# Inverting the softmax sums of couples 6 to 23 as 14 columns over 128 partitions instead of as 448 columns over 128

## The chip, the core and the metric

The kernel runs on one core of a Trainium2 chip. A core has five engines that run their own instruction streams side by side: TensorE (PE, the matrix multiplier, which writes to PSUM only), VectorE (DVE), ScalarE (ACT), GpSimd (POOL) and SyncE (SP), which here does nothing but issue DMAs. Every stream is in order: an instruction that waits for a semaphore holds back all that stand behind it on the same engine. The metric is the device time of one execution in microseconds (us).

## The reference

Attention over 8 batches, 12 heads, 448 positions and head size 64, with q and k normalised by their root mean square, followed by a two-layer network on the 3584 rows (model width 768, inner width 2048):

```python
rms = np.sqrt(np.mean(x * x, axis=-1, keepdims=True) + 1e-06)   # for q and for k, times a gain
scores = (1 / np.sqrt(64)) * np.matmul(q_n, k_n.transpose(0, 1, 3, 2))
attn = np.exp(scores - max);  attn = attn / (sum(attn) + 1e-09)
x = matmul(attn, v)                     # rows (b, s), columns (h, d)
h = x @ w_in                            # 768 -> 2048
out = (h * (1 / (1 + np.exp(-h)))) @ w_out   # 2048 -> 768
```

All in float32. The kernel doesn't subtract the maximum where the gains bound the scores; that is the path that runs (`bounded`).

## The kernel before, in words

**Couples.** Four heads of one batch are a couple (24 couples, 3 per batch; `GROUP` = 6 couples are two batches). For couple c, `visit(c)` computes scores for 128 keys at a time (L752), exponentials on ScalarE (L757), and products with v (L789) that add up in two PSUM banks, `av0` and `av1`, of which there is one buffer each. `between(c)` then prepares the next couple (transposes or `flip` of q and k) and fills TensorE's time with matmuls of the first layer of the network, for the two batches that were finished before: `fill(...)` takes them from a generator (`halves_in`, L963), product by product. Each product of 448 columns goes to a PSUM bank, of the pool `ps_mm` (name `mm`, two buffers) or, by turns, of the pool with the scores (name `sc`, two buffers of two banks). VectorE or ScalarE takes it out; with two buffers, a product into `mm` can start only when the product before the last one in `mm` has been taken out.

**Sums.** The softmax's sum over keys is a matmul with ones. From couple 6 on VectorE first adds the exponentials of the key blocks onto those of block 0 (`add`, L803), so that TensorE has one term left: 4 matmuls of 32 output rows (L832), which give the four heads' sums, each repeated over 32 of the 128 partitions. In couples 6 and 10 (`FULL`) the block of left-over keys wasn't added by VectorE; it is a second term of 4 matmuls.

**Reciprocals.** `invert(half)` (L841) takes the reciprocal of 128 x 224 sums from PSUM, twice, into `r[0]`; `spread` copies it to `r[1]` (L847), and 4 DMAs from SBUF to SBUF (L850, on SP) exchange halves, so that `r[i]` has the factor of each of the 128 rows of x of pair i. `divide(c, sums)` (L863) multiplies the two `av` banks by `r[0]` and `r[1]`, two instructions, and so frees the banks.

**Order.** Nothing but the order in the program decides. For couples 6, 7, 8, 9, 11, 17 and 23 the sums and reciprocals stand in `between(c)`, and `divide(c, sums)` stands in `visit(c + 1)`, ahead of the first product with v of couple c + 1. In the other couples from 10 on (`LAGGED`) the sums stand at the end of `between(c)`, the reciprocals in `visit(c + 1)`, x is copied out undivided (L1526) and divided in `between(c + 1)`. The pieces of `prompt` are put between the fill's products: the first one ahead of them, one more after each product. SP issues everything in order too: loads of q, k and v, of the weights, the stores of the layer's result to DRAM (L1002), and the reciprocals' DMAs.

After couple 23 the rest of the first layer and then the second layer follow, without attention.

## Time and profile before

| | us |
|---|---|
| median of 3 runs | 1294.37 |
| lowest, highest | 1294.12, 1294.78 |
| span of the profiled execution | 1294.6 |
| PE busy | 1283.5 |
| DVE busy | 971.4 |
| ACT busy | 504.3 |
| POOL busy | 363.5 |
| attention with the first layer beside it (up to the last product with v) | about 711 of the span |

The page gives per engine its busy time, the chain of work that ended last and groups of like instructions. Timelines give for one engine the start in us from the span's beginning, the time taken, engine and line, operation, output and inputs, and how often in a row; in brackets how long the engine stood idle ahead of it and who released it. A PE row counts two records for each matmul in float32, so a term of the sums (4 matmuls) is x8. A row of SPq is the issue of DMAs; landing comes later. The granted TensorE clock was 0.999 over the execution.

### The profile page before, as it was taken

The numbers are of one execution on the slowest core, as the hardware profiler recorded it, in microseconds if no ns is written. First come the engines' busy times: TensorE is split into PE (matmuls) and PEld (weight loads), VectorE is DVE, ScalarE is ACT, GpSimd is POOL, SyncE is SP. The second block draws the span as 40 slices with busy tenths as digits, with TensorE's granted clock in tenths as the row PEclk, the third lists the DMA queues.
The fourth block names the chain that finished last, engine by engine and source line by source line (L and its number), as shares of the span: only waits on it lengthen the run. The fifth ranks groups of instructions, "written<-read, shape, count | busy, mean of one in ns | idle before, by whom it ended". The sixth has DMA issues, their size and how long they took to land.

```text
span 1294.6 us, 19931 instructions
## 1 busy us (share of the span) xinstructions
PE 1283.5 (99%) x7212; PEld 840.7 (65%) x7212; DVE 971.4 (75%) x1672; ACT 504.3 (39%) x880; POOL 363.5 (28%) x221
## 2 busy tenths in 40 slices
PE   9999999999999999999999999999999999999998
PEld 4444454444444454444544555559999999999998
DVE  6898878868666558666555886798978787878785
ACT  7967666645555554554543344310001000000000
POOL 6765454543344344343311344400000000000000
PEclk9999999999999999999999999999999999999999
DMA  9675347434444444444411466312332313141411
GB/s 232 174 193 136 104 124 197 95 83 102 112 94 91 119 91 102 108 93 93 107 50 69 149 204 219 117 66 88 100 94 86 113 67 129 51 133 48 141 39 40
DMA packets 266160, 144.15 MB, mean 111 GB/s; under 512 B 203748, under 2 KB 249956, under 8 KB 266052
## 3 DMA queue, kind: packets, MB, share of 16 engines
q1 hardware_dynamic: 265424, 141.68, 39.8%
q8 instruction: 59, 0.97, 0.3%
q0 software_dynamic: 320, 0.90, 0.2%
q14 instruction: 49, 0.40, 0.1%
q10 hardware_dynamic: 308, 0.20, 0.1%
HBM read 95.36 MB, written 41.29 MB: 106 GB/s over the span
## 4 chain that ended last, share of the span: by engine, by line
PE 97%; DVE 1%; POOL 1%; issue 0%; ACT 0%; DMA 0%; SPq 0%; ACTq 0%; DVEq 0%; POOLq 0%
PE alone L1285 23%; PE mm L963 21%; PE sc L963 11%; PE av L789 10%; PE sc L752 10%; PE mm L1285 8%; PE alone L963 7%; PE alone L1323 2%; PE mm L832 2%; PE mm L1323 1%; PE sc L643 1%; PE sc L832 1%; PE sc L674 0%; DVE work L912 0%; POOL rms L503 0%
## 5 line engine op out<-in xcount | busy, mean ns | idle before, releaser
L757 ACT ACTIVATE work<-sc,rms 128x448 f32<-128x448 f32 x318 | 182.0, 635 | 98.0 <-PE sc L752 85.7
L752 PE MATMUL sc<-work 64*64 64x448 f32 x1344 | 169.4, 543 | 1.0 <-ACT work L653 0.6
L789 PE MATMUL av<-work,rows 64*64 64x448 f32 x1272 | 155.5, 540 | 1.2 <-DVE x L1514 0.9
L963 PE MATMUL mm<-x,W 128*128 128x448 f32 x366 | 149.1, 542 | 0.0
L963 PE MATMUL mm<-sums_x,W 128*128 128x448 f32 x348 | 142.4, 542 | 0.0
L803 DVE TENSOR_TENSOR work<-work 128x896 f32<-128x896 f32 (+1 forms) x110 | 118.3, 1105 | 28.6 <-PE av L789 28.1
L530 POOL DMA_DIRECT2D out_dram<-x x2 | 1.2, 592 | 443.5 <-DVE x L912 443.5
L503 POOL TENSOR_TENSOR rms<-rms,minus_half 128x14 f32<-128x14 f32 (+4 forms) x40 | 97.4, 2437 | 86.8 <-DVE rms L499 83.3
L963 PEld LDWEIGHTS mm<-x,W 128*128 128x128 f32 x366 | 68.5, 190 | 70.3 <-issue 64.8
L1285 PE MATMUL alone<-W,rows 128*128 128x192 f32 x610 | 113.0, 326 | 0.0
L963 PEld LDWEIGHTS mm<-sums_x,W 128*128 128x128 f32 x348 | 65.1, 190 | 68.1 <-issue 62.5
L789 PEld LDWEIGHTS av<-work,rows 64*64 64x64 f32 x1272 | 65.9, 132 | 62.8 <-issue 19.3
L752 PEld LDWEIGHTS sc<-work 64*64 64x64 f32 x1344 | 60.4, 132 | 63.3 <-ACT work L757 25.3
L1285 PEld LDWEIGHTS alone<-W,rows 128*128 128x128 f32 x610 | 101.4, 190 | 0.0
L963 PE MATMUL sc<-x,W 128*128 128x448 f32 x246 | 99.6, 541 | 0.0
L984 POOL TENSOR_TENSOR stage<-parts,stage 128x448 f32<-128x448 f32 x31 | 39.8, 1285 | 169.2 <-ACT stage L983 168.9
L722 POOL TENSOR_TENSOR rms<-rms,minus_half 128x28 f32<-128x28 f32 x15 | 72.6, 4842 | 48.9 <-DVE rms L719 47.8
L963 PEld LDWEIGHTS sc<-x,W 128*128 128x128 f32 x246 | 46.4, 190 | 47.0 <-issue 46.7
L1285 PE MATMUL alone<-W,work 128*128 128x192 f32 x382 | 72.2, 326 | 0.0
L1295 ACT COPY rows<-alone 128x192 f32<-128x192 f32 x33 | 10.5, 318 | 141.5 <-PE alone L1285 136.7
L1285 PEld LDWEIGHTS alone<-W,work 128*128 128x128 f32 x382 | 63.8, 190 | 0.0
L1116 ACT ACTIVATE stage<-stage 128x896 f32<-128x896 f32 x63 | 56.8, 945 | 17.1 <-DVE stage L912 16.9
(267 smaller groups left out, 2312.8 us busy)
## 6 DMA issues: line engine op xcount, KB each, us to landing
hidden<-stage SPq DMA_DIRECT2D x63, 448.0 KB, 2.9
work<-hidden SPq DMA_DIRECT2D x21, 1024.0 KB, 5.1
rows<-in_moe_w_out_dram SPq DMA_DIRECT2D x32, 384.0 KB, 3.7
W<-in_moe_w_in_dram SPq DMA_DIRECT2D x22, 512.0 KB, 5.3
x<-hidden SPq DMA_DIRECT2D x7, 1024.0 KB, 6.1
rows<-in_q_dram SPq DMA_DIRECT2D x120, 56.0 KB, 2.2
rows<-in_k_dram SPq DMA_DIRECT2D x120, 56.0 KB, 2.3
rows<-in_k_dram SPq DMA_DIRECT2D x60, 96.0 KB, 2.6
```

The costliest lines, as they stand in the source:

```text
L503: nc.gpsimd.tensor_tensor(out=t, in0=t, in1=half, op=ALU.pow)
L722: nc.gpsimd.tensor_tensor(out=f, in0=f, in1=minus_half.to_broadcast([P, n]), op=ALU.pow)
L752: nc.tensor.matmul(two[ds(half * D, D), h, 0:S], keys[rows, ts(half, D)], qT[rows, pair, :], start=True, stop=True,)
L757: nc.scalar.activation(left_weights(c)[:, h] if j == LEFT else weights(c, j)[:, i, h], two[:, h, 0:S], AF.Exp, scale=norm.column(c, i, h, j),)
L789: nc.tensor.matmul(sums[i][ds(h * D, D), :], v, w, start=(j == 0 and step == 1), stop=(j == LEFT - 1 and step == 1),)
L803: nc.vector.tensor_tensor(out=total, in0=total, in1=more, op=ALU.add)
L832: nc.tensor.matmul(t[ds(h * D + i * n, n), :], ones[:, which + i if which else 0], left_weights(c)[:, h] if which else w()[:, i, h], start ...
L963: nc.tensor.matmul(t, self.left(name, s), self.right(name, s), start=s == ends[0], stop=s == ends[1])
L984: nc.gpsimd.tensor_tensor(out=done[1, 2], in0=u2, in1=p5, op=ALU.add)
L1116: nc.scalar.activation(t, t, AF.Silu)
L1285: nc.tensor.matmul(t, x[:, i], y, start=i == ORDER[0], stop=i == ORDER[-1])
L1323: nc.tensor.matmul(o, a[:, 2 * i + m, t], right_one(name, i)[:, m], start=n == 0, stop=n == len(steps) - 1,)
```

## The change

For c >= 6, `sum_up` gives other pieces. `gather`: ScalarE copies all sums, 128 x 448, from PSUM to `r[0]`, and 4 DMAs take one partition of each group of 32 (448 values, one head) and lay it out as 32 partitions x 14 in a new tile `spot`; the four heads fill 128 partitions. `invert_all`: VectorE takes the reciprocal of `spot`, 128 x 14; one DMA writes it to a DRAM tile `totals` (two of them, by turns), and 4 DMAs read it back, each one head's 448 values repeated over 64 partitions, into `r[0]` and `r[1]`. The second term of couples 6 and 10 goes; VectorE adds the left-over keys there too. Couples 0 to 5 stay as they were.

```diff
-    FULL = (GROUP, SOON - 1)
+    totals = [dram.tile([4, S], F32, name=f"totals{i}") for i in range(2)]
+    spot = mem.tile([P, 4 * S // P], F32, name="spot")
...
-        if c in FULL:
-            terms.insert(0, (1, None))
...
-        yield [lambda: invert(0), lambda: (invert(1), spread())]
+        def gather():
+            nc.scalar.copy(r[0], t)
+            rows = r[0].rearrange("(n p) s -> n p s", n=4)[:, 0]
+            for n in range(4):
+                dst = spot[ts(n, P // 4)]
+                nc.sync.dma_start(dst, rows[n : n + 1].rearrange("n (p e) -> n p e", p=P // 4))
+
+        def invert_all():
+            d = totals[c % 2]
+            nc.vector.reciprocal(out=spot, in_=spot)
+            nc.sync.dma_start(d.rearrange("n (p e) -> (n p) e", p=P // 4), spot)
+            for i in range(2):
+                for h in range(2):
+                    source = d[2 * h + i : 2 * h + i + 1].to_broadcast([D, S])
+                    nc.sync.dma_start(r[i][ts(h, D)], source)
+
+        if c >= GROUP:
+            yield [gather, invert_all] if c in LAGGED else [gather, lambda: None, invert_all]
+        else:
+            yield [lambda: invert(0), lambda: (invert(1), spread())]
...
             if LATE - 1 <= c < NC - 1:
-                reciprocals += [lambda: flip(c + 1, "k"), gain]
+                reciprocals[1] = lambda: flip(c + 1, "k")
+                reciprocals.append(gain)
...
-        late = add(c, LEFT - 1) if c >= GROUP else []
-        if c >= GROUP and c not in FULL:
-            late += add(c, LEFT)
+        late = add(c, LEFT - 1) + add(c, LEFT) if c >= GROUP else []
```

Three places show how this moves instructions. Names: `rows` is the ring of loaded q, k and v, `W` the weights, `stage` and `parts` hold products on their way out, `work` holds `r`.

SP in couple 8, before: the loads of k by rows, the exchange of the reciprocals, the eight loads of k by quarters (which wait for `flip`), then weights and stores.

```order
L287 DMA rows<-in_k_dram 128x3x64 x2
L289 DMA rows<-in_k_dram 64x2x64
L850 DMA work<-work 32x448 x4
L255 DMA rows<-in_k_dram 32x14x32 x8
L88 DMA x_173<-in_moe_w_in_dram 128x512
L1002 DMA hidden<-stage 128x896 x2
```

The same place after the change:

```order
L287 DMA rows<-in_k_dram 128x3x64 x2
L289 DMA rows<-in_k_dram 64x2x64
L862 DMA spot<-work 32x1x14 x4
L255 DMA rows<-in_k_dram 32x14x32 x8
L867 DMA totals_172<-spot 128x14
L871 DMA work<-totals_172 64x448 x4
L88 DMA x_175<-in_moe_w_in_dram 128x512
L1020 DMA hidden<-stage 128x896 x2
```

Four DMAs have become nine, and the eight loads now stand between the first four and the last five. In couples 11 and 17 the order is the same; in couple 9 the two stores to `hidden` stand in between as well; in couple 7 the eight loads stand ahead of all nine.

VectorE in couple 7, second half, before: the two reciprocals and the copy, one piece of weights, the sum of squares (L705), and the first two products taken out of PSUM (L912).

```order
L841 RECIPROCAL work<-sc 128x224 x2
L847 COPY work<-work 128x448
L126 TENSOR_SCALAR W<-W 128x512
L129 TENSOR_SCALAR W<-W 128x512
L133 SCALAR_TENSOR_TENSOR W<-W 128x512
L705 TENSOR_REDUCE rms_61<-rows 128x28
L912 TENSOR_TENSOR parts<-sc,parts 128x448
L912 TENSOR_TENSOR stage<-mm,stage 128x448
```

The same place after the change:

```order
L126 TENSOR_SCALAR W<-W 128x512
L129 TENSOR_SCALAR W<-W 128x512
L133 SCALAR_TENSOR_TENSOR W<-W 128x512
L866 RECIPROCAL spot<-spot 128x14
L930 TENSOR_TENSOR parts<-sc,parts 128x448
L706 TENSOR_REDUCE rms_61<-rows 128x28
L930 TENSOR_TENSOR stage<-mm,stage 128x448
```

The small reciprocal, which needs the four gathers landed, stands ahead of three instructions that didn't wait for a DMA before.

VectorE in couple 6, first half, before: additions of exponentials, one piece of weights, and a product taken out of PSUM.

```order
L803 TENSOR_TENSOR work<-work 128x896 x2
L126 TENSOR_SCALAR W<-W 128x512
L129 TENSOR_SCALAR W<-W 128x512
L133 SCALAR_TENSOR_TENSOR W<-W 128x512
L912 TENSOR_TENSOR parts<-mm,parts 128x448
```

The same place after the change:

```order
L804 TENSOR_TENSOR work<-work 128x896 x2
L804 TENSOR_TENSOR work<-work 64x896 x2
L126 TENSOR_SCALAR W<-W 128x512
L129 TENSOR_SCALAR W<-W 128x512
L133 SCALAR_TENSOR_TENSOR W<-W 128x512
L930 TENSOR_TENSOR parts<-mm,parts 128x448
```

Two additions of 64 x 896 now stand ahead of the product. TensorE's own order is the same before and after, but for the 8 matmuls that go.

## The prediction

> **What bounds the kernel now.** I read the page first, for the engine that is never free, then TensorE's waits, then the timelines of the couples that the change touches, SP and VectorE beside TensorE.

> ```profile
> span 1294.6 us, 19931 instructions
> ...
> PE 97%; DVE 1%; POOL 1%; issue 0%; ACT 0%; DMA 0%; SPq 0%; ACTq 0%; DVEq 0%; POOLq 0%
> ```

> The second line is the chain that ended last, by engine: 97% of the span is TensorE following TensorE. How little it waits is in the view of waits, which for TensorE has 8 rows, of which the first and the last are:

> ```profile
> PE idle L412 <- POOL ident masks.py:199: 1.4, 1, 1.4
> ...
> PE sc L643 <- DVE rows L518: 0.2, 1, 0.2
> ```

> The eight add up to 4.8 us, and only few tenths of that lie beyond the start. So a faster VectorE can give next to nothing by itself; the change can win only what it takes off TensorE, and it loses whatever makes TensorE wait. What has to be asked is how long each new chain of DMAs is, and what stands behind it.

> **What it takes off TensorE.** The sums of couple 6, with two terms, and of couple 7, with one:

> ```profile
> 135.48 1.71 PE L832 MATMUL sc<-work,ones 128*32 128x448 f32 x16
> ...
> 169.56 0.96 PE L832 MATMUL sc<-work,ones 128*32 128x448 f32 x8
> ```

> A term costs 1.71 - 0.96 = 0.75 us. Couples 6 and 10 lose one each: **-1.5 us**.

> **What it takes off and puts on the others.** By groups, and one pair of the added additions as it stands in couple 23:

> ```profile
> L841 DVE RECIPROCAL work<-mm 128x224 f32<-128x224 f32 x24 | 37.0, 1547 | 4.1 <-PE mm L832 4.1
> ...
> L983 ACT COPY stage<-sc 128x448 f32<-128x448 f32 x10 | 5.3, 528 | 20.2 <-PE sc L963 20.2
> ```
> ```profile
> 692.01 2.20 DVE L803 TENSOR_TENSOR work<-work 64x896 f32<-64x896 f32 x2
> ```

> In each of 18 couples VectorE loses two reciprocals of 1.55 us and a copy; the reciprocal of 14 columns is 14/224 of 1.55, 0.1 us, say 0.2 with its overhead. By the waits above this saves TensorE nothing. ScalarE gets a copy out of PSUM, 0.53 us each.

> **The new chain.** The trace has no such DMAs, so I build it from the nearest rows: the exchange that goes, a k load of 96 KB (read from DRAM) and stores to DRAM.

> ```profile
> L850 SPq DMA_DIRECT2D work<-work x74: 513/583/1280, 112.5 to 703.6; - x74
> ...
> DMA to landing us min/median/max: 1.9/2.0/3.8
> ```
> ```profile
> rows<-in_k_dram SPq DMA_DIRECT2D x60, 96.0 KB, 2.6
> ...
> out_dram<-work SPq DMA_DIRECT2D x4, 120.0 KB, 2.1
> ...
> out_dram<-work SPq DMA_DIRECT2D x6, 48.0 KB, 4.2
> ```

> An issue takes SP 0.58 us, four 2.4 us; a small DMA lands 2.0 us after its issue. Four gathers issued from T: the fourth is issued at T + 1.8 and landed at T + 3.8; the reciprocal is done at T + 4.0. The write to DRAM lands 2.0 later (between 1.9 and 4.2, the last row; I take 2.0, as it is nearer in size to the exchange). The four reads (64 x 448 values, 112 KB) wait for it on SP; the fourth is issued 1.8 later and lands after 2.4, between 2.1 and 2.6. So `r` is complete **6.2 us after the write's issue**, 10.2 after T where nothing stands between. The old exchange needed 1.8 + 2.0 after the copy.

> [...]

> Now each place where something waits for this. A divide that starts at D frees `av0` and `av1` for the next products with v. Couple 7's shows the slack:

> ```profile
> 184.59 1.16 DVE L863 TENSOR_TENSOR x<-av,work 128x448 f32<-128x448 f32 x2 [1.34 <-PE av L789]
> ```
> ```profile
> 185.88 0.56 PE L789 MATMUL av<-work,rows 64*64 64x448 f32 x4
> ```

> The first product is at D + 1.3, the one into the second bank 0.38 later, and the divide's second half takes 0.62: it can start at D + 1.0 without holding TensorE.

> Couple 7. SP, VectorE and TensorE:

> ```profile
> 173.31 4.19 SPq L255 DMA_DIRECT2D rows<-in_k_dram  x8
> ```
> ```profile
> 176.51 1.08 DVE L705 TENSOR_REDUCE rms<-rows 128x28 f32<-128x896 f32 x1
> 177.50 0.61 DVE L912 TENSOR_TENSOR parts<-sc,parts 128x448 f32<-128x448 f32 x1
> 178.03 0.61 DVE L912 TENSOR_TENSOR stage<-mm,stage 128x448 f32<-128x448 f32 x1
> ```
> ```profile
> 179.57 0.92 PE L963 MATMUL mm<-x,W 128*128 128x448 f32 x2
> ```

> The gathers stand behind the eight loads: T = 177.5, landed 181.3, reciprocal done 181.5. VectorE holds until then, and behind it stand the three instructions of 0.61, 1.08 and 0.61 us: 183.8. The matmul at 179.57 needs the bank that the third of them empties. **+4.2 us**. `r` is complete at 187.7, against 185.6 + 4.2: no more.

> Couple 8:

> ```profile
> 206.00 0.60 SPq L289 DMA_DIRECT2D rows<-in_k_dram  x1
> ...
> 209.88 4.18 SPq L255 DMA_DIRECT2D rows<-in_k_dram  x8
> ```
> ```profile
> 216.51 1.16 DVE L863 TENSOR_TENSOR x<-av,work 128x448 f32<-128x448 f32 x2 [1.31 <-PE av L789]
> ```

> T = 206.6; gathers to 209.0, eight loads to 213.2, then the write: `r` at 219.4, allowed 217.5. **+1.9**.

> Couple 9, with the two stores between as well:

> ```profile
> 235.56 0.60 SPq L289 DMA_DIRECT2D rows<-in_k_dram  x1
> ...
> 242.32 1.19 SPq L1002 DMA_DIRECT2D hidden<-stage  x2
> ```
> ```profile
> 248.42 1.16 DVE L863 TENSOR_TENSOR x<-av,work 128x448 f32<-128x448 f32 x2 [1.34 <-PE av L789]
> ```

> 236.2 + 2.4 + 4.2 + 1.2 = 244.0; `r` at 250.2, allowed 249.4. **+0.8**.

> Couples 11 and 17, in the order of couple 8:

> ```profile
> 301.75 0.60 SPq L289 DMA_DIRECT2D rows<-in_k_dram  x1
> ```
> ```profile
> 312.84 1.16 DVE L863 TENSOR_TENSOR x<-av,work 128x448 f32<-128x448 f32 x2 [0.28 <-PE av L789]
> ```
> ```profile
> 501.48 0.60 SPq L289 DMA_DIRECT2D rows<-in_k_dram  x1
> ```
> ```profile
> 512.72 1.16 DVE L863 TENSOR_TENSOR x<-av,work 128x448 f32<-128x448 f32 x2 [0.28 <-PE av L789]
> ```

> 302.35 + 2.4 + 4.2 + 6.2 = 315.1, allowed 313.8: **+1.3**. 502.1 + 12.8 = 514.9, allowed 513.7: **+1.2**.

> Couple 6. VectorE is full here, and the two additions stand ahead of a product that TensorE waits for:

> ```profile
> 130.39 1.37 DVE L126 TENSOR_SCALAR W<-W 128x512 f32<-128x512 f32 x1
> ...
> 132.87 0.62 DVE L912 TENSOR_TENSOR parts<-mm,parts 128x448 f32<-128x448 f32 x1
> ...
> 151.18 1.16 DVE L863 TENSOR_TENSOR x<-av,work 128x448 f32<-128x448 f32 x2 [1.29 <-PE av L789]
> ```
> ```profile
> 174.97 0.43 DVE L126 TENSOR_SCALAR W<-W 128x512 f32<-128x512 f32 x1
> ```
> ```profile
> 133.87 0.92 PE L963 MATMUL mm<-sums_x,W 128*128 128x448 f32 x2
> ```
> ```profile
> 145.99 0.86 SPq L1002 DMA_DIRECT2D hidden<-stage  x2
> ```

> 2.2 us more would end that product at 135.7 instead of 133.5. The first of the three weight steps behind the additions took 1.37 us beside a busy GpSimd and 0.43 in couple 7, and starts 2.2 later, when GpSimd is done: about 1.2 us later in all (0 to 2.2). **+1.2**, which eats that couple's 0.75. Its `r`: the write goes out behind the stores, at 146.9 at the latest, complete 153.1, allowed 152.2 plus the 0.4 that TensorE is late by then; the reciprocals that go let the weights and so the stores go earlier, so 0 (0 to 0.5).

> Couple 10 costs nothing: its additions stand where VectorE idles. The lagged couples and the last one:

> ```profile
> 675.88 1.16 ACT L757 ACTIVATE work<-sc,rms 128x448 f32<-128x448 f32 x2 [1.24 <-PE sc L752]
> ```
> ```profile
> 696.53 1.15 DVE L863 TENSOR_TENSOR x<-x,work 128x448 f32<-128x448 f32 x2
> ...
> 711.25 1.16 DVE L863 TENSOR_TENSOR x<-av,work 128x448 f32<-128x448 f32 x2 [1.10 <-PE av L789]
> ```

> Couple 22: gathers from 677.6 (exponentials, then the copy), `r` at 687.8, wanted at 696.5. Couple 23: copy after the divide that ends at 697.7, T = 698.2, `r` at 708.4, wanted at 711.25. Nothing in either; they are hidden by the matmuls of the first layer, and cost only if the chain took over 3 us more.

> **Sum.** -1.5 + 4.2 + 1.9 + 0.8 + 1.3 + 1.2 + 1.2 = +9.1 us, on a span of 1294.6, 0.2 above the median of the runs. On the median, 1294.37: **1303.5**.

> **The rivals.**

> *Slow hops.* If the write to DRAM takes the 4.2 us of the 48 KB stores, `r` is 2.2 later: 8.8 in couples 8, 9, 11 and 17, some 1.4 in couple 6, 0.1 in couple 7: 1313.8. For it speaks that row; against it the other stores, 2.1. Chance 0.15. [...]

> *Short hops.* If write and reads take under 4.3 us instead of 6.2, couples 8, 9, 11 and 17 are free: -1.5 + 1.2 + 4.2, 1298.3. Against it: no row lands under 1.9, and the four issues alone are 2.4. Chance 0.13.

> *Not slower: no wait decides.* One mechanism, the gathers are issued before the eight loads hold them up: SP, freed of L850's waits, runs ahead, so that couple 7's reciprocal is done by 177 and `r` early everywhere. That needs T by 173 in couple 7. Then only the terms count: 1292.9, or 1294.1 with couple 6's additions. Against it: the gathers stand behind the loads in the order, and SP issued these without a gap. Chance 0.10.

> **How the numbers follow.** My forecast, 0.62, has 1300 to 1308 as its own range by the bounds above. For 8 in 10 I reach down into the short hops and up to the slow ones: 1296 to 1313. About 0.2% is what a measurement of this kernel can tell from no change, that is 1291.8 to 1297.0. Slower: the forecast, the slow hops and most of the short ones, 0.85. The same: the last rival and a little of the short hops, 0.13. Faster by more needs 2.6 us, and the terms are 1.5: 0.02.

> **What would show it.** In the new profile: L832 in couples 6 and 10 with x8; a TensorE idle of about 4 us in couple 7's second half, put down to VectorE or to DMA into `spot`; in couples 8, 9, 11 and 17 waits of VectorE's divide for DMA into `work`, with 1 to 2 us of TensorE behind each; 1 us in couple 6; nothing in the lagged couples or in couple 23. It is wrong if these landings are not near 2 us, or if TensorE doesn't need the bank in couple 7.

## The result and the profile after

The changed kernel takes 1325.09 us (median of 5 runs, 1321.37 to 1328.36) against 1294.49 (1294.12 to 1294.78): 1.0238 times as long, 95% interval 1.0222 to 1.0255, **30.6 us slower**. The forecast was 1303.5, its range 1296 to 1313. The sign was right, the size was not: the loss is over three times the 9.1 us of the sum.

The page of the profiled execution (1328.29 us, of which 1326.5 are the span) first: the span, TensorE's busy time, the granted clock by slices, and the chain that ended last.

```profile
span 1326.5 us, 20023 instructions
...
PE 1298.6 (98%) x7196; PEld 840.3 (63%) x7196; DVE 910.6 (69%) x1640; ACT 511.3 (39%) x898; POOL 363.6 (27%) x221
...
PEclk9999889999999999999999999999999999999999
...
PE 86%; DMA 4%; SPq 3%; DVE 2%; ACT 2%; issue 1%; POOL 1%; ACTq 0%; DVEq 0%; POOLq 0%
```

Two things stand out. The chain is TensorE for 86% instead of 97%: DMA, SP and VectorE have come into it, so there are new waits. And TensorE is **busy** for 15.1 us more than before (1298.6 against 1283.5), though it runs 16 matmul records less. Two slices of its clock are at 8 tenths, and the mean granted clock is 0.991 instead of 0.999.

The waits of TensorE, in total per releaser (us in total, times, longest); these are the new rows:

```profile
PE av L790 <- DVE x L881: 11.4, 9, 2.2
PE mm L981 <- DVE stage L930: 3.9, 1, 3.9
PE mm L981 <- DVE parts L930: 1.7, 1, 1.7
...
PE mm L981 <- ACT stage L992: 0.7, 1, 0.7
```

17.7 us, none of which stood in the profile before. In TensorE's timeline the places are these (start, us; in brackets the idle time ahead and the releaser):

```profile
134.21 1.02 PE L981 MATMUL mm<-sums_x,W 128*128 128x448 f32 x2 [1.73 <-DVE parts L930]
...
154.42 1.28 PE L790 MATMUL av<-work,rows 64*64 64x448 f32 x4 [2.12 <-DVE x L881]
...
189.78 1.86 PE L981 MATMUL mm<-x,W 128*128 128x448 f32 x2 [3.86 <-DVE stage L930]
...
235.16 0.59 PE L790 MATMUL av<-work,rows 64*64 64x448 f32 x2 [1.67 <-DVE x L881]
...
269.34 0.97 PE L790 MATMUL av<-work,rows 64*64 64x448 f32 x4 [2.24 <-DVE x L881]
271.40 1.01 PE L790 MATMUL av<-work,rows 64*64 64x448 f32 x2 [1.09 <-DVE x L881]
...
338.12 0.97 PE L790 MATMUL av<-work,rows 64*64 64x448 f32 x4 [1.42 <-DVE x L881]
...
543.47 2.22 PE L790 MATMUL av<-work,rows 64*64 64x448 f32 x6 [1.81 <-DVE x L881]
```

In this order they are couple 6's additions, couple 6's divide, couple 7's bank, and the divides of couples 8, 9 (two rows), 11 and 17. Six of these seven places were named in the prediction with a wait of their own; couple 6's divide was put at nothing.

What lies behind each wait shows in windows of TensorE (from:to, length, busy and records, **granted clock**, DMA share, GB/s):

```profile
154.95:161.78 6.83, 6.51 (x34) 0.50 0.07 15
189.08:195.91 6.83, 6.13 (x30) 0.50 0.25 70
225.00:235.00 10.00, 8.19 (x69) 1.00 0.62 135
271.00:274.41 3.41, 3.01 (x16) 0.50 0.06 14
339.27:342.68 3.41, 3.14 (x18) 0.50 0.08 18
544.07:547.48 3.41, 3.41 (x18) 0.50 0.13 28
```

Behind five of the seven waits TensorE ran at half clock, 0.50, for 3.41 us or for twice that. Reckoned from that clock as half the work, a stretch of 3.41 us costs it 1.7, and the five rows lose 3.4 + 3.4 + 3 x 1.7 = **12 us** at most (11 if only the 22.2 us count in which it was busy there), an estimate. That is why busy time grew: in the timeline above, the two records at 189.78 take 1.86 us at half clock; the same two took 0.92 before. The starts of the five stretches lie 34.13, 81.92, 68.27 and 204.80 us apart, which is 10, 24, 20 and 60 times 3.413: in this execution half clock set in on a grid of 3.413 us, not at the moment in which a wait began or ended (in couple 9 1.66 us after TensorE had started again at 269.34, in couple 7 0.70 us before it did at 189.78).

So of the 31.9 us between the two spans, waits are 17.7 and half clock some 12; the terms give back 1.5, and the first 100 us, whose code is the same, have 1.2 us less idling in this execution (TensorE busy for 96.63 us instead of 95.42). About 5 us remain that neither view places.

### The profile page after: what moved, and what is told of

Read it like the earlier page. It is cut to its first block, busy times and chain, and to the rows that moved or that the text cites. A ratio compares the mean times of both kernels' runs of the same rounds, so it can differ in the third digit from the quotient of the medians.

```text
span 1326.5 us, 20023 instructions
## 1 busy us (share of the span) xinstructions
PE 1298.6 (98%) x7196; PEld 840.3 (63%) x7196; DVE 910.6 (69%) x1640; ACT 511.3 (39%) x898; POOL 363.6 (27%) x221
## 4 chain that ended last, share of the span: by engine, by line
PE 86%; DMA 4%; SPq 3%; DVE 2%; ACT 2%; issue 1%; POOL 1%; ACTq 0%; DVEq 0%; POOLq 0%
PE alone L1303 22%; PE mm L981 16%; PE av L790 9%; PE sc L981 9%; PE sc L753 9%; PE mm L1303 8%; PE alone L981 7%; PE alone L1341 2%; PE mm L831 2%; SPq L255 1%; DMA work<-totals 1%; DMA totals<-spot 1%; PE mm L1341 1%; SPq L871 1%; ACT stage L1134 1%
## 5 line engine op out<-in xcount | busy, mean ns | idle before, releaser
L753 PE MATMUL sc<-work 64*64 64x448 f32 x1344 | 181.7, 558 | 1.1 <-ACT work L654 0.6
L790 PE MATMUL av<-work,rows 64*64 64x448 f32 x1272 | 170.5, 558 | 11.7 <-DVE x L881 11.4
L804 DVE TENSOR_TENSOR work<-work 128x896 f32<-128x896 f32 (+1 forms) x114 | 125.0, 1126 | 43.9 <-PE av L790 43.3
L1002 POOL TENSOR_TENSOR stage<-parts,stage 128x448 f32<-128x448 f32 x31 | 38.9, 1255 | 185.6 <-ACT stage L1001 176.8
L1313 ACT COPY rows<-alone 128x192 f32<-128x192 f32 x33 | 10.5, 318 | 141.3 <-PE alone L1303 141.3
```

What stands on the lines that cost most here:

```text
L753: nc.tensor.matmul(two[ds(half * D, D), h, 0:S], keys[rows, ts(half, D)], qT[rows, pair, :], start=True, stop=True,)
L790: nc.tensor.matmul(sums[i][ds(h * D, D), :], v, w, start=(j == 0 and step == 1), stop=(j == LEFT - 1 and step == 1),)
L804: nc.vector.tensor_tensor(out=total, in0=total, in1=more, op=ALU.add)
L1002: nc.gpsimd.tensor_tensor(out=done[1, 2], in0=u2, in1=p5, op=ALU.add)
```

## The experiments

Each run's time stands beside runs of the kernel before on the same chip; in a diff, + and - are against the kernel that its text names.

### The additions alone

```diff
-    FULL = (GROUP, SOON - 1)
+    FULL = ()
```

> The kernel before with one line changed: the second term of couples 6 and 10 goes, VectorE adds the left-over keys; the reciprocals stay the old ones. Theory 'waits and half clock' (TensorE's waits at the places where something waits for the new chain, and stretches at half TensorE clock that follow them, make the whole loss): -1.5 us for the terms, +1.9 for the product of couple 6 that is taken out later: 1294.4 to 1295.5, no stretch at half clock; 1296.7 if this one wait sets one off. Rival 'additions' (the additions on a full VectorE in couple 6 make what follows late): over 1305.

1295.13 (1294.76 to 1295.64, 10 runs), before 1294.65; ratio 1.0003, interval 0.9994 to 1.0013. TensorE's wait is there as in the changed kernel, with no half clock behind it (mean clock of the profiled execution 0.999):

```profile
133.63 1.02 PE L963 MATMUL mm<-sums_x,W 128*128 128x448 f32 x2 [1.74 <-DVE parts L912]
```

+0.5 us fits the wait of 1.7 less 1.5 for the two terms, though the interval has no change in it as well. The rival "additions", which asked for over 1305, falls.

### The new chain where nothing waits for it

```diff
+    NEW = [c for c in range(GROUP, NC) if c in LAGGED or c == NC - 1]
...
-        if c >= GROUP:
+        if c in NEW:
             yield [gather, invert_all] if c in LAGGED else [gather, lambda: None, invert_all]
```

> The new chain only in the 11 lagged couples and couple 23; couples 6, 7, 8, 9, 11 and 17 keep the old reciprocals and exchange, couples 6 and 10 keep the second term. Theory 'waits and half clock': nothing waits for the chain there, so 1294.5, within 0.5. Rival 'traffic' (the added DMAs and bytes, 9 for 4 in a couple, slow the other transfers wherever they are): 12 of 18 couples still have them, so 12/18 of the loss, 1310 to 1316.

1294.45 (1293.97 to 1295.89), before 1294.65; ratio 0.9998, interval 0.9989 to 1.0008. From 100 to 720 us of the span TensorE is as busy as before (619.56 us, before 619.63), with 48 of the 72 reads in place:

```profile
100.00:720.00 620.00, 619.56 (x3393) 1.00 0.44 108
```

Where nothing waits for it the chain cost nothing that 0.1% could show; "traffic" falls. The six couples 6, 7, 8, 9, 11 and 17 carry the whole loss.

### One of the six

```diff
+    NEW = [c for c in range(GROUP, NC) if c == 17]
```

> The new chain in couple 17 alone, everything else as before. Theory 'waits and half clock': the 1.8 to 2.5 us of waiting seen there and one stretch of 3.4 us at half clock, 1.7 us more: 1298.0 to 1298.7 where the stretch comes, 1296.3 to 1297.0 in executions where it doesn't. Rival 'waits alone', as the prediction had it: 1295.7, all runs alike. Rival 'traffic': one couple of 18, 1296.2, no half clock.

1296.87 (1296.09 to 1299.42, 11 runs), before 1294.65; ratio 1.0019, interval 1.0010 to 1.0028. The single runs say more than the median. Six lie at 1296.1 to 1296.9 with a mean clock of 0.999 to 1.000, four at 1298.3 to 1298.5, all with 0.997; one, the profiled one, at 1299.42 with 0.998. The same wait costs some 1.7 us, and in four executions 2 more, in which the clock is lower. "Waits alone" can't give these two groups. But no trace shows the second group: the profiled execution has full clock behind couple 17, with waits of 0.8 and 0.7 us, and what it took longer lies in the first 100 us, whose code is the same (TensorE busy for 95.72 us there, 97.32 in lagged_new). That half clock made the second group is read from the mean clocks alone.

```profile
514.00:520.00 6.00, 4.54 (x40) 1.00 0.26 61
```

### Work in the waits

The changed kernel, with matmuls that nobody reads ahead of the first product with v:

```diff
+    def keep_clock(n):
+        if n:
+            for k in range(2):
+                unread = ps_mm.tile([P, BANK], F32, name="mm")[:, 0:P]
+                for _ in range((n + k) // 2):
+                    nc.tensor.matmul(unread, ident, ident, start=True, stop=True)
...
+        keep_clock({7: 8, 9: 5, 10: 9, 12: 6, 18: 6}.get(c, 0))
         weigh(c, 0, 1)
```

> The changed kernel with 5 to 9 matmuls of 128 x 128 whose result nobody reads, ahead of the first product with v of couples 7, 9, 10, 12 and 18, where TensorE waited for the divide. Theory 'waits and half clock': the waits' time stays, taken by useless matmuls, but the half-clock stretches behind these four or five places go (6.8 + 3.4 + 3.4 + 3.4 us at half clock, worth 8.5): 1315 to 1319, with one stretch left, in couple 7. Rival 'another cause' (the clock falls for something else than TensorE's idling): 1325 or more, five stretches as before.

1322.55 (1320.79 to 1323.63), before 1294.65: a miss, 3.5 us above what I expected and hardly below the changed kernel. The windows show why:

```profile
156.00:163.00 7.00, 7.00 (x60) 1.00 0.19 45
183.00:191.00 8.00, 4.67 (x30) 0.79 0.25 61
...
268.00:273.00 5.00, 5.00 (x38) 0.66 0.00 1
...
538.00:545.00 7.00, 6.05 (x59) 1.00 0.14 32
```

Half clock behind couples 6, 11 and 17 is gone and couple 7's and 9's have one stretch each: 1.7 + 1.7 us lost instead of 12. Couple 9's wait was only 1.35 us here. But the matmuls were busy for 9.4 us, and the waits at the divides fell only from 11.4 to 5.3; the filling was partly added to the waits. It needed a cleaner case, which follows.

### The same waits without any DMA

The kernel before, in which VectorE does some divides four times over (the same product again):

```diff
-                    divide(c - 1, sums)
+                    for _ in range(4 if c - 1 in (8, 9, 11, 17) else 1):
+                        divide(c - 1, sums)
```

> The kernel before, in which VectorE does the divide of couples 8, 9, 11 and 17 four times over (the same values again), and no DMA is changed: each holds TensorE for about 3 x 1.16 us less a slack of 1.0, 2.5 us. Theory 'waits and half clock' (a wait of TensorE of some 2 us is enough to bring a stretch at half clock, whoever causes it): 10 us of waits and some 3.4 us at half clock behind most of the four places, 1308 to 1313, mean clock 0.993 to 0.997. Rival 'another cause' (the half clock comes with the new DMAs, not with TensorE's idling): 1304 to 1305, all at 0.999.

1312.29 (1312.10 to 1312.46), before 1294.36; ratio 1.0139, interval 1.0123 to 1.0155. The wait, then windows of 3.41 us on the grid on which this execution's stretches start (255.02 and 528.09, 80 times 3.413 apart), for couples 8, 9 and 17:

```profile
PE av L789 <- issue: 9.9, 4, 2.5
```
```profile
214.06:217.47 3.41, 2.57 (x28) 1.00 0.87 276
217.47:220.88 3.41, 1.78 (x18) 1.00 1.03 418
251.61:255.02 3.41, 1.03 (x10) 1.00 0.36 74
255.02:258.43 3.41, 3.41 (x24) 0.50 0.00 0
524.67:528.09 3.42, 0.95 (x10) 1.00 0.21 48
528.09:531.50 3.41, 3.41 (x24) 0.50 0.02 5
```

Four waits of 2.5 us each ("issue", since the profile shows no releaser), three of them with 3.4 us of half clock behind: 5.1 us lost. No DMA was added. The windows show what sets the one spared place of four apart: couple 8's wait falls into two of them, with 0.84 and 1.63 us of idling (3.41 less the busy time), while the waits of couples 9 and 17, of the same length, lie in one window (2.38 and 2.47 us idle), and the next has a clock of 0.50. With 9.9 of waits and 5.1 of half clock, 2.9 of the 17.9 us stand in neither view. The same edit with three divides:

> As the run named stall, with three divides in place of four: the wait at each of the four places is 1.16 us shorter, 1.3 us by the 2.5 measured there. Theory 'waits and half clock' with a need for some 2 us of idling: 17.9 - 4 x 1.16 = 13.3 less the half clock that goes: 1302.5 to 1304.5, no half clock (mean clock 0.999). Rival 'any wait brings it': three stretches as before, 1307 to 1308, mean clock 0.995.

1302.84 (1301.85 to 1305.68), before 1294.35; ratio 1.0065, interval 1.0045 to 1.0086. Four waits of 1.4 us, and no half clock in the profiled execution (mean clock 0.999). One of the four runs, the longest (1305.68), has a mean clock of 0.997 where the others have 0.999, so a stretch in it can't be excluded. The loss of 8.5 us is again 2.9 more than the waits: each of the four late divides cost some 0.7 us beyond the wait that is shown, and the 5 us of the changed kernel may be of this kind, which was not tried.

```profile
PE av L789 <- issue: 5.6, 4, 1.4
```
```profile
249.00:260.00 11.00, 9.60 (x84) 1.00 0.26 51
```

And with four divides, and 9 matmuls of 128 x 128 in each wait, put in as above:

> As the run named stall (four divides in couples 8, 9, 11 and 17), and TensorE does 9 matmuls of 128 x 128 that nobody reads, 2.4 us, in each of the four waits of 2.5 us. Theory 'waits and half clock' (the clock falls since TensorE idles, not since a divide is late): the lateness stays, the half clock goes: 5.1 us less than stall, 1306.5 to 1308.5, mean clock 0.999. Rival 'it comes with a late divide': 1312 or more, three stretches as before.

1307.13 (1306.42 to 1308.56), before 1294.35; ratio 1.0097, interval 1.0078 to 1.0115: **5.2 us less than stall, by adding useless work**. The waits are filled and the clock stays, 0.999 in all four runs:

```profile
251.31 2.60 PE L1555 MATMUL mm<-ident 128*128 128x128 f32 x18
253.84 1.11 PE L789 MATMUL av<-work,rows 64*64 64x448 f32 x6
```
```profile
251.00:255.00 4.00, 3.94 (x33) 1.00 0.34 68
255.00:259.00 4.00, 4.00 (x45) 1.00 0.02 4
```

The divides are as late as in stall; only the idling is gone. So in these runs the half clock came with the idling of TensorE (0.50 behind it in stall, 1.00 here), not with the DMAs and not with the lateness.

### The reciprocal ahead of the eight loads

```diff
-            yield [gather, invert_all] if c in LAGGED else [gather, lambda: None, invert_all]
+            first = [gather, invert_all]
+            yield first if c in LAGGED or c >= LATE - 1 else [gather, lambda: None, invert_all]
...
-                reciprocals[1] = lambda: flip(c + 1, "k")
-                reciprocals.append(gain)
+                reciprocals += [lambda: flip(c + 1, "k"), gain]
```

> The changed kernel with one order changed: in couples 8, 9, 11 and 17 the small reciprocal, the write and the four reads stand ahead of the eight loads of k (in couple 9 ahead of the two stores too) instead of behind them. Theory 'waits and half clock': the factors are complete some 10.5 us after the gathers' first issue, before the divides want them; the four waits and the half clock behind three of them go, 2.7 + 5.4 + 4.4 + 4.6 = 17 us by the profile: 1307 to 1310, half clock left behind couples 6 and 7. Rival 'a new wait' (SP holds the eight loads back by 6 us, and what needs k comes late): 1315 to 1330, TensorE waiting for DMA into rows or for what normalises k. Rival 'slow hops' (the chain is too long even without the loads between): waits of over 1 us stay at these divides.

1314.57 (1314.25 to 1317.52), before 1294.18; ratio 1.0162, interval 1.0147 to 1.0178: of the 17 us that I expected, about 10 came back (a loss of 20.4 us beside 30.6). The waits at the divides of couples 8, 9, 11 and 17 are gone. What came instead stands in couple 8, on VectorE and then on TensorE:

```profile
221.83 0.24 DVE L866 RECIPROCAL spot<-spot 128x14 f32<-128x14 f32 x1 [5.87 <-DMA spot<-work]
```
```profile
224.14 3.90 PE L982 MATMUL mm<-x,W 128*128 128x448 f32 x6 [2.08 <-DVE stage L931]
```

The reciprocal holds VectorE until the gathers land, as in couple 7, and TensorE waits for a bank; a window from 224 to 229 us shows a clock of 0.66, one more stretch. A new wait, but not the one I named: not the loads of k, but the engine that waits for the gathers.

In the next run the sums and gathers of couple 7 also stand ahead of its eight loads (`reciprocals[0]()` is called before `transpose_k(c + 1)` there):

> As in the run named order, and in couple 7 the sums and the four gathers stand ahead of the transposes and so of the eight loads. Theory 'waits and half clock': VectorE's small reciprocal no longer waits 8 us, the 3.9 us of TensorE at its bank and the half clock behind it go: 6.5 to 7.5 us less than the run named order, 1300 to 1303. Rival 'a new wait' (the loads, later by the gathers, hold up couple 9's k, or the sums, earlier on TensorE, wait for VectorE's additions): less than half of that.

1311.33 (1308.91 to 1311.91), before 1294.18; ratio 1.0125, interval 1.0110 to 1.0141: 3.2 us less than order, not 7. Couple 7's wait of 3.9 us is gone; couple 8's wait for a bank is there still, 2.1 us, and the mean clock of the profiled execution is 0.996 where order's is 0.994. But couple 7's divide is now late, which it never was in the changed kernel:

```profile
184.58 0.42 SPq L867 DMA_DIRECT2D totals<-spot  x1
187.93 2.41 SPq L871 DMA_DIRECT2D work<-totals  x4
```
```profile
192.13 2.25 PE L790 MATMUL av<-work,rows 64*64 64x448 f32 x6 [1.81 <-DVE x L882]
```

SP reads back 3.35 us after the write, which stands right behind the eight loads. The 3.9 us on VectorE had hidden that couple 7's chain was too long as well.

### The old exchange in couples 6 and 7

```diff
+    NEW = [c for c in range(GROUP, NC) if c not in (6, 7)]
```

> The changed kernel with the old reciprocals and exchange in couples 6 and 7 alone; the second terms stay dropped. Theory 'waits and half clock': the prices add up place by place, so the 6.5 us behind couple 6's divide and the 7.1 in couple 7 go: 1310 to 1313, half clock left behind couples 9, 11 and 17. Rival 'the state spreads' (a late couple makes the next ones late, so that the places are not independent): the later waits shrink or grow by over 2 us, time outside 1308 to 1315.

1314.85 (1310.78 to 1320.18), before 1294.18; ratio 1.0148, interval 1.0131 to 1.0164. Outside what I expected, by its spread: the four runs are 1310.78 at a clock of 0.996, 1313.64 and 1316.05 at 0.995, and 1320.18 at 0.993. In the profiled one half clock stands behind couple 8's divide too, whose wait is 2.06 us there and was 1.67 in the changed kernel without it; timeline and window of that place:

```profile
225.51 0.92 PE L792 MATMUL av<-work,rows 64*64 64x448 f32 x2 [2.06 <-DVE x L885]
```
```profile
225.00:230.00 5.00, 4.49 (x28) 0.66 1.03 391
```

The waits at couple 6's divide and couple 7's bank are gone, as expected, but a gain can't be added up to the microsecond: the mean clock of this one kernel lies between 0.993 and 0.996 in its four runs.

### Fewer bytes in the reads

```diff
-                    source = d[2 * h + i : 2 * h + i + 1].to_broadcast([D, S])
-                    nc.sync.dma_start(r[i][ts(h, D)], source)
+                    source = d[2 * h + i : 2 * h + i + 1, 0 : S // 4].to_broadcast([D, S // 4])
+                    nc.sync.dma_start(r[i][ts(h, D), 0 : S // 4], source)
```

> The changed kernel with the four reads cut to the first 112 of 448 columns, 28 KB each for 112; it leaves out the factors of the other columns, so the division is only right in a quarter of x. Theory 'bytes set the read's landing' (112 KB took 2.8 to 4.3 us to land, against the 2.4 of the prediction): the fourth lands some 2 us after its issue, the waits at the divides of couples 6, 8, 9, 11 and 17 shrink by about 1 us each and half clock goes at some: 1314 to 1320. Rival 'a fixed delay' (the landing takes 3 us whatever the size): 1321 to 1328 as the changed kernel.

Beside it the changed kernel ran once more:

> The changed kernel once more, to set the two kernels beside it on the same chip and to see its spread. Theory 'waits and half clock': times between 1320 and 1329 that go up as the mean granted clock goes down, some 1.7 us for each stretch of 3.4 us at half clock. Rival 'another cause' (the spread has nothing to do with the clock): no such order.

short_reads takes 1317.58 (1317.23 to 1323.12), and again, on the same chip, 1323.28 (1319.48 to 1323.43); before 1294.36. Again's shortest run has the highest clock: 1323.43 and 1323.17 at 0.991, 1323.39 at 0.993, 1319.48 at 0.995. The reads' issues in short_reads (KB each, median us to landing, which is 3.0 in again):

```profile
work<-totals SPq DMA_DIRECT2D x72, 28.0 KB, 2.6
```

A quarter of the bytes takes 0.4 us off a landing, not 1, and yet 5.7 us off the median of the kernel (one of its four runs, 1323.12 at 0.991, is as long as again's): the waits at the divides fall from 9.9 to 7.8, the longest of them from 2.2 to 1.9, and the mean clock of the profiled execution goes from 0.991 to 0.996, which comes to some 13 us less at half clock (an estimate: 0.005 x 1316 us / 0.5).

### Two versions near the kernel before

best has the `NEW` of lagged_new; drop10 has all old reciprocals. In both the second term goes in couple 10 alone:

```diff
-    FULL = (GROUP, SOON - 1)
+    FULL = (GROUP,)
```

> The new chain only in the 11 lagged couples and couple 23, and the second term of couple 10 alone dropped. Theory 'waits and half clock': nothing waits, TensorE has 0.75 us less to do than in the run named lagged_new (1294.45): 1293.5 to 1294.0. Rival 'the additions in couple 10 cost': 1294.4 or more.

> The kernel before with the second term of couple 10 alone dropped, VectorE adding the left-over keys there; all reciprocals are the old ones. By the term's price TensorE has 0.75 us less and nothing waits: 1293.4 to 1293.9, as the run named best. If the new chain in the lagged couples had a gain of its own, best would lie below this by over 0.3; if it had a cost, above.

best took 1293.78 (11 runs) beside 1294.18: ratio 0.9996, interval 0.9987 to 1.0005. drop10 took 1293.49 (11 runs) beside 1294.36: 0.9995, 0.9986 to 1.0004. Both medians lie below the kernel before, by 0.4 and 0.9 us for a term priced at 0.75, neither by more than its interval. There is no sign that the new chain gains anything of its own where it costs nothing.

## Why the prediction was wrong

**Right.** The bound (TensorE's order, never free), the sign, and the places: couple 6's additions, couple 7's VectorE, the divides of 8, 9, 11 and 17; nothing in the lagged couples and couple 23, and nothing for additions in couple 10. Couple 7's hold was forecast at 4.2 and is 3.86. A term is worth what it was priced at in the trace (couple 6's sums take 0.96 us after the change, 1.71 before); as a time, drop10's 0.9 us is within its noise. One reading was loose without harm to the 9.1 us: the span of an execution is some 1.8 us shorter than its time (1326.5 beside 1328.29), so the profile before, with a span of 1294.6, would be of an execution some 2 us over the median, not 0.2.

**Wrong: a wait was priced at its length.** Every term of the sum stopped where TensorE starts again. In the profiled execution it starts again at half clock, or falls to it within 2 us, at five of seven places, for 12 us. The runs showed the cause in kernels with no DMA changed: waits of 2.5 us brought a stretch in three places of four, the same lateness with TensorE kept at work none. The length of the wait alone doesn't decide. Couple 6's additions (1.73 us) and couple 8's 0.30 + 1.67 brought none, 1.81 in couple 17 and 1.42 + 0.45 in couple 11 one each. It sorts better, though not cleanly, by the grid of 3.413 us. In the profiled execution of the changed kernel these are all windows of that grid, behind the first 5 us and ahead of the last matmul, in which TensorE idled for more than 1 us (length less busy time):

```profile
131.05:134.47 3.42, 1.69 (x5) 1.00 0.00 0
151.53:154.95 3.42, 1.30 (x12) 1.00 0.64 168
185.67:189.08 3.41, 0.24 (x1) 1.00 0.05 4
233.45:236.87 3.42, 1.75 (x22) 1.00 0.93 362
267.59:271.00 3.41, 0.97 (x4) 1.00 0.46 118
335.85:339.27 3.42, 1.83 (x16) 1.00 0.59 160
540.65:544.07 3.42, 1.61 (x16) 1.00 0.58 158
```

Behind the 2.12, 3.17, 2.44 and 1.81 us of idling the next window has a clock of 0.50; of the 1.73, 1.67 and 1.59 us only the last has half clock behind it. In stall's rows 2.38 and 2.47 us have it and 1.63 has not. And the changed kernel's last matmuls leave 1.96 us of idling in a window, with full clock in the next:

```profile
1318.89:1322.31 3.42, 1.46 (x9) 1.00 0.61 174
1322.31:1325.72 3.41, 0.00 (x0) 1.00 0.12 31
```

What decides in between, and why some stretches are double, stays open.

The profile before has a clock of 0.999 and no idling of over 1.4 us in its couples, but its last 6 us could have raised the question: TensorE's last matmul ends at 1288.4, and after almost 4 us of idling the clock is 0.50.

```profile
1290.00:1292.00 2.00, 0.00 (x0) 1.00 0.36 99
1292.30:1294.50 2.20, 0.00 (x0) 0.50 0.03 11
```

**Wrong: the size of two hops.** The reads were taken at 2.4 us from the last issue, between 2.1 and 2.6, from a k load and a store. They landed after 2.8 to 4.3, median 3.0, and the write after 1.4 to 5.3, median 1.7 (first the reads in the page's view of issues, KB each and median us to landing; then the line of the write's own view):

```profile
work<-totals SPq DMA_DIRECT2D x72, 112.0 KB, 3.0
```
```profile
DMA to landing us min/median/max: 1.4/1.7/5.3
```

Short_reads shows that bytes were the smaller part of it (2.6 us with a quarter of them). The write was taken at 2.0 everywhere, and that was the size in couples 8, 11 and 17 (1.8 to 2.0), but not where it stands right behind the two stores to `hidden`. SP in couples 6 and 9:

```profile
143.82 0.85 SPq L1020 DMA_DIRECT2D hidden<-stage  x2
144.90 0.71 SPq L867 DMA_DIRECT2D totals<-spot  x1
150.25 1.79 SPq L871 DMA_DIRECT2D work<-totals  x3
```
```profile
260.33 0.90 SPq L1020 DMA_DIRECT2D hidden<-stage  x2
261.32 0.62 SPq L867 DMA_DIRECT2D totals<-spot  x1
264.79 3.25 SPq L871 DMA_DIRECT2D work<-totals  x4
```

The first read waits for the write on SP, 5.35 us behind its issue in couple 6 and 3.5 in couple 9. The prediction let couple 6's write go out at 146.9 and land at 148.9; it went out 2 us earlier and landed at 150.2. That is the divide which was put at nothing, and cost 2.4 us of waiting and 3.4 of half clock. The landings say what the write waited for: the second store was issued at 144.28 and 260.86 and landed after 5.8 and 3.7 us, at 150.1 and 264.6, and the write some 0.2 us behind it. In couples 8 and 11 it landed as closely behind the last load of k, at 228.4 after 228.2 and at 334.0 after 333.8. In the changed kernel the write was read back after 1.9, 3.5, 2.0 and 1.8 us in couples 8, 9, 11 and 17; in the run order, where it stands ahead of those loads and stores in these four, the median landing of all 18 writes is 1.4 us instead of 1.7. So the queue ahead of such a small DMA belongs into its price.

**The terms side by side** (us: forecast; waits of the profiled execution; lost to half clock): couple 6's additions 1.2; 1.7; 0. Couple 6's divide 0; 2.4; 3.4. Couple 7 4.2; 3.9; 3.4. Couple 8 1.9; 2.0, and 0.7 at L992; 0. Couple 9 0.8; 3.3; 1.7. Couple 11 1.3; 1.9; 1.7. Couple 17 1.2; 1.8; 1.7. Sums: 10.6 of waits forecast, 17.7 measured, 12 on top.

**The rivals.** "Slow hops" came nearest, 1313.8: the write is late, but behind stores (5.3 us in couple 6), not in itself (1.4 us in order, median). "Short hops" and "not slower" fell. The step on couple 7 had the hold right and what stands behind it wrong ("no more"): with VectorE's hold taken away (early7) the divide waits, and only 3.2 of some 7 us came back.

## What to carry to other kernels

Where one engine is never free, price a wait of its own at more than its length: here 17.7 us of waits had some 12 us of half clock behind them, by estimate. Ask what the clock does behind a wait, and look twice at one near 2 us: of the changed kernel's windows with 1.6 to 1.8 us of idling, two had half clock behind them and two had not. Filling such waits with useless work gained 5.2 us in stall_filled and, where the work was partly added to the waits, hardly anything in filled. A wait that is shown can hide the next one on the same path, as couple 7's did, so that taking it away brings back only the difference (3.2 of some 7 us); work the slack out again without it. An operation that leaves an engine with time to spare gained nothing here (61 us less VectorE), and the longer chain of small DMAs was free in lagged_new (1294.45 beside 1294.65), where couple 23's result is wanted 13 us after the copy of the sums (698.2 and 711.25 in the profile before).
